# A chunked delta rule with two MoE layers on one core: four MoE pieces in place of the unused products at the first change of set, and y right behind S

## The chip, the cores and the metric

One core of a Trainium2 chip runs the whole program. The metric is the device time of one execution in microseconds (us), as the median of several runs. Its engines are TensorE (PE; PEld is its weight load), VectorE (DVE), ScalarE (ACT), GpSimd (POOL) and SyncE (SP), whose queue issues most DMAs here.

## The reference

Three stages follow each other. The first is a delta-rule attention over 4 batches x 8 heads, 768 positions of 48 values each:

```
k_n = k / (norm(k) + 1e-6);  state = 0
for t in range(S):
    y[t]  = q[t] @ state
    state = state + beta[t] * outer(k_n[t], v[t] - k_n[t] @ state)
```

Its output becomes x with 3072 rows (tokens) of 384 values. The first MoE stage is `h = ((x @ w1) * (x @ w2)) @ w3 @ w_out` with an inner width of 1024. The second is `solu = h * softmax(h)` with `h = x @ w_in`, a normalisation over the 1024 columns, and a product with `w_out`. All inputs are float32.

## The kernel before

**Chunks and sets.** The recurrence is cut into chunks of 64 positions. There are 48 chunks (64 positions of all heads of one batch), worked on in pairs (the same positions of two batches), one pair a step: 24 steps (the loop at L783), c = 2s. Four steps (8 chunks) form a set; there are six sets, 0 to 5. For every set an inverse of unit triangular matrices is needed, which VectorE builds with 62 small dependent operations between two rounds of transpositions (`invert`, L322, and `invert_end`, L343). The inverse of set n+1 is started in the second step of set n (`start_inverse`, turn 5) and goes on four operations a turn.

**A step.** `chain_u(c)` (L433) multiplies the merged inverse with V and the state and writes U over V in `X`. `chain_s(c)` (L449) adds the pair to the state in PSUM (`pst`) and copies the state into the next slot of `X`. `chain_y(c)` (L475) makes the outputs of the pair from `X` and `QA`, rounds them into the two halves of `xb`, the input of the first MoE stage, and after every second pair issues six DMAs (L499) that move the last 16 head rows of `xb` to their place. `load_v` (L421) brings V of a later pair into the same slot of `X`, which is a ring of two pairs. `merge_1`, `merge_2` and `merge_3` (L359 to L418) turn an inverse into the matrices `TW` of a pair; the functions `norm`, `prep_t` and `prep_g` (L241 to L306) normalise, transpose and multiply keys and queries of the next set. At a change of set `enter` (L762) runs the merges of the first pair of the new set.

**MoE pieces.** The first MoE stage is cut in 12 blocks of 256 tokens (`moe_block`, L566). A block is a generator with 14 pieces: 8 pieces of 18 matmuls into `pab` (128x128 by 128x256; L579), each followed by two ScalarE and two VectorE operations (L586 to L589), and 6 pieces of 12 matmuls into `px` (L603). `pab` has two PSUM buffers. `fill(x)` (L750) adds x to a counter that is capped at 3 and issues a piece for each whole unit; while the block's input isn't there yet, it issues none. A block j is let in when `y_done` reaches 4(j+1); block 0 when it reaches 6 (L738). `fill` is called eight times a step with `FT[k_]` (k_ is the step in its set; the eight calls are `turn(0)` to `turn(7)`, four ahead of `chain_s` and four behind it), and three times with `FB` = 1.4 around the merges in `enter`. What is left when the 24 steps are done runs in a tail (L882), with the conversion of the last weights between (`wog`).

**Order.** TensorE's order is the program's (`manual_schedule` at L780); the other engines' order is set by the framework's planner. `ps_prep` is a pool of four PSUM buffers that the products of the chain, the merges, the key products and y share. At the first change of set, `awake(24)` (L745) issues 24 products of the identity with itself, which nobody reads; a profile shows each as two matmuls.

The lines of the old order are these:

```
        chain_u(c)
        if s:
            chain_y(c - 2)
            y_done[0] = c
            if RX <= c + 2 < NCH:
                load_v(c + 2)
```

Of the kernel before, what the change touches and what calls it, by code (L numbers as in the profile page):

```python
# [8 lines left out]
F32 = mybir.dt.float32  # L9
# [11 lines left out]
def kernel(  # L21
# [15 lines left out]
    nc = tc.nc  # L37
# [7 lines left out]
    NCH = B * CPB  # L45
# [5 lines left out]
    TB = 256  # L51
# [3 lines left out]
    RQ, RT, RX = 16, 4, 4  # L55
# [5 lines left out]
    FB = 1.4  # L61
    FT = (0.68, 0.72, 0.8, 0.78)
    P0, C0 = 4, 24
    LO = 2
    WO, WB = 2, 15
    CPP = 2 * CPB
# [18 lines left out]
    ps_ab = ps_moe_stack.enter_context(tc.tile_pool(name="ps_ab", bufs=2, space=PSUM, side="right"))  # L85
# [7 lines left out]
    ident = const.tile([128, 128], F32, name="ident")  # L93
# [133 lines left out]
    def chunk_at(c):  # L227
        return c // CPP * 2 + c % 2, (c % CPP) // 2 * C
# [125 lines left out]
    def xcopy(c, lim):  # L354
        return nc.scalar.copy if c < lim or c >= CA and c % SETC >= SETC // 2 else nc.vector.tensor_copy
# [65 lines left out]
    def load_v(c):  # L421
        b, s0 = chunk_at(c)
        xs = slice(c % RX, c % RX + 2)
        t = v[b:b + 2].rearrange("b (p e) s d -> e s b p d", e=2)
        for h in range(2):
            nc.sync.dma_start(out=X[64 * h:64 * h + 64, xs, :, h, 0:D], in_=t[1 - h, s0:s0 + C])
        if c % CPP < 2:
            nc.gpsimd.memset(X[64:KA, xs, :, 0, 0:D], 0.0)
            nc.gpsimd.memset(X[0:D, xs, :, 1, 0:D], 0.0)
# [19 lines left out]
    def chain_s(c):  # L449
        if c % CPP >= CPP - 2:  # L450
            return
        first = c % CPP == 0
        if first:
            s_t[0] = ps_one.tile([128, 2, NP, D], F32, tag="s", name="pst")
        st, xs, xn = s_t[0], c % RX, (c + 2) % RX
        ks, sk = kst[c % RQ * 2 // RQ], c % (RQ // 2)
        for cc in range(2):

            with tc.issue_after(s_t[1].ins) if first and cc else nullcontext():
                for p in range(NP):  # L460
                    for h in range(2):
                        r = slice(64 * h, 64 * h + 64)
                        o = 64 * (1 - h)
                        mm = nc.tensor.matmul(  # L464
                            st[o:o + D, cc, p, :], ks[r, sk + cc, p, :], X[r, xs + cc, p, h, 0:D],
                            start=(first and not cc and p == 0), stop=True, skip_group_check=True,
                        )
                        if first and not cc and p == 0:
                            s_t[1] = mm
        nc.scalar.copy(out=X[64:KA, xn:xn + 2, :, 0, 0:D], in_=st[64:KA])  # L470
        conv(2 * C0, xcopy(c, CA)(out=X[0:D, xn:xn + 2, :, 1, 0:D], in_=st[0:D]))
# [3 lines left out]
    def chain_y(c):  # L475
        (qa, qs), xs = qa_of(c % RQ), c % RX
        py = ps_prep.tile([128, 2, NP, C], F32, tag="prep", name="py")
        for cc in range(2):
            for p in range(NP):
                for h in range(2):  # L480
                    o = 64 * (1 - h)
                    nc.tensor.matmul(  # L482
                        py[o:o + 64, cc, p, :], X[0:kr[h], xs + cc, p, h, :], qa[0:kr[h], qs + cc, p, h, :],
                        start=True, stop=True, skip_group_check=True,
                    )
        j = c // CPT
        if c % CPT == 0:
            xb_t[j] = moe.tile([128, 2, NP, TB], F32R, tag="xb", name="xb", bufs=2)
        xb = xb_t[j]
        hi, lo = (  # L490
            xb[:, a].rearrange("r p (b k t) -> r b p k t", b=2, k=CPT // 2)[:, :, :, c % CPT // 2, :]
            for a in range(2)
        )
        nc.scalar.copy(out=hi, in_=py)
        conv(2 * C0, nc.vector.tensor_tensor(out=lo, in0=py, in1=hi.bitcast(F32), op=ALU.subtract))
        if c % CPT == CPT - 2:
            for m in range(NM):
                for o in (0, 64):
                    nc.sync.dma_start(  # L499
                        out=xb[o + D:o + 64, :, m, :].bitcast(F32),  # L500
                        in_=xb[o + 16 * m:o + 16 * m + 16, :, NP - 1, :].bitcast(F32),
                    )
# [199 lines left out]
    def conv(x, ins=None):  # L702
        acc[0] += x
        if acc[0] < 1:
            return
        with (tc.issue_after(ins.ins) if ins is not None and c_done[0] >= CA else tc.issue_after(held[0].ins) if held[0] is not None else nullcontext()):
            while acc[0] >= 1:
                next(wg, None)
                acc[0] -= 1
# [24 lines left out]
    y_done = [0]  # L734
# [7 lines left out]
    mg = moe_all()  # L742
    owed = [0.0]

    def awake(n):  # L745
        for _ in range(n):
            pd = ps_ab.tile([128, 2, TB], F32, tag="ab", name="pd")
            nc.tensor.matmul(pd[:, 0, 0:128], ident, ident, start=True, stop=True, skip_group_check=True)

    def fill(x):  # L750
        owed[0] = min(owed[0] + x, 3.0)
        while owed[0] >= 1.0:
            if next(mg, "wait") == "wait":
                return
            owed[0] -= 1.0
# [27 lines left out]
    for s in range(NSTEP):  # L783
        c, n, k_ = 2 * s, s // PER, s % PER
        nxt = n + 1 < NSET
        if c == CD:
            drain(wg)
        b = (n + 1) * PER
        jobs = {}
        if nxt and k_ == 0:  # L790
            jobs = {
                1: lambda: prep_t(b + 1), 3: lambda: norm(b + 2),
                5: lambda: prep_t(b + 2), 7: lambda: norm(b + 3),
            }
        elif nxt and k_ == 1:
            jobs = {1: lambda: prep_t(b + 3), 5: lambda: start_inverse(n + 1)}
        elif n + 2 < NSET and k_ == PER - 1:
            jobs = {4: lambda: norm(b + PER), 7: lambda: first_keys(b + PER)}

        def turn(t):  # L800
            if t in jobs:
                jobs[t]()
            fill(FT[k_])
            for _ in range(IV):
                next(inv_gen_[0], None)

        chain_u(c)
        if s:
            chain_y(c - 2)
            y_done[0] = c  # L810
            if RX <= c + 2 < NCH:
                load_v(c + 2)
        if k_ < 2:
            merge_2(c + 2)
        if k_ == 1:
            merge_1(c + 4)
        if nxt and k_ < 2:
            prep_g(b + 2 * k_)
        for t in range(4):
            turn(t)  # L820
        chain_s(c)
        c_done[0] = c
        if k_ < PER - 1:
            merge_3(c + 2)
        if nxt and k_ < 2:
            prep_g(b + 2 * k_ + 1)
        if k_ == 0:
            merge_1(c + 4)
        if k_ == 1:
            merge_2(c + 4)  # L830
        for t in range(4, 8):
            turn(t)
        if k_ == PER - 1 and nxt:
            drain(inv_gen_[0])
            invert_end(n + 1)
            if not n:
                awake(24)
            enter(c + 2, FB)
        if c == NCH - SETC:
            prep_stack.close()  # L840
            pbw = ctx.enter_context(tc.tile_pool(name="pbw", bufs=1, side="right"))
            assert RQ == 2 * SETC and NSET % 2 == 0
            late = at.tile([128, 2 * DFF + 4 * DM], F32R, tag="QA0", name="late")
            wis = [pbw.tile([128, 2, DFF], F32R, name=f"wis{m}") for m in range(NM - 1)]
            wis.append(late[:, 0:2 * DFF].rearrange("p (a x) -> p a x", a=2))
            wig = weights_i(pbw, wis)
        if c >= NCH - SETC:
            for _ in range(NM * DFF // 256 * 6 // (SETC // 2) + 1):
                next(wig, None)
    chain_y(NCH - 2)  # L850
    y_done[0] = NCH
    while shared[0]:
        next(mg)
    pinned.__exit__(None, None, None)
# [40 lines left out]
    def b_h(i):  # L895
# [17 lines left out]
        p2 = pb2.tile([128, 1], F32, tag="p2", name="p2")  # L913
        sc = pb3.tile([128, 1], F32, tag="sc", name="sc", bufs=LO + 1)
        e = pb2.tile([128, DFF], F32, tag="e", name="e")
# [23 lines left out]
    def b_t(i):  # L939
        cen, sc = cen_t.pop(i)  # L940
        ln = pb2.tile([128, 2, NF, 128], F32R, tag="ln", name="ln", bufs=LO)
        for g in range(NF // 4):
# [21 lines left out]

    for i in range(NT128 + LO):
        if i < NT128:
# [3 lines left out]
            for _ in range(WB):  # L970
                next(wog, None)
        if i == LO:
            drain(wog)
        if i == NT128:
            b_o(i - LO)
            b_t(i - 1)
        else:
            if 0 <= i - LO:
                b_o(i - LO)
# [33 lines left out]
```

## Time and profile before

| | |
|---|---|
| median of 3 runs | 903.52 us (902.31 to 903.79) |
| the profiled execution | 905.32 us, span 903.6 us |
| TensorE busy | 827.2 us (92% of the span) |
| VectorE busy | 603.1 us (67%) |
| ScalarE busy | 451.1 us (50%) |
| mean granted TensorE clock | 0.954 of full |
| 24 steps of the recurrence | about 108 to 640 us of the span |
| tail of the first MoE stage | about 640 to 676 us |
| second MoE stage | about 676 us to the end |

Times of rows are microseconds from the start of the span, names are `out<-in`, and `L579` is line 579 of the kernel. A row of a timeline merges instructions of one line that follow each other; the bracket at its end is the time that the engine sat idle ahead of it, and what ended that. "PEclk" is the clock that TensorE was granted, as a share of full speed: 1.00 is 2.4 GHz and 0.50 is 1.2 GHz.

### The profile page before, as it was taken

Reading aid. Unit: us, or ns where it says so; the run is one execution under the profiler, and the core shown is the slowest. Engines: PE = TensorE matmul, PEld = TensorE weight load, DVE = VectorE, ACT = ScalarE, POOL = GpSimd, SP = SyncE. Lnnn points to the kernel's source line nnn. Section 1 sums busy time; section 2 is a strip of 40 time slices with the busy share of each in tenths; the row PEclk is TensorE's granted clock in tenths of the full one; section 3 lists DMA queues with packets and bytes.
Section 4 is the critical chain, followed back from the end, with each engine's and each line's share of the span. In section 5 each row is a group of like instructions: output and inputs, shape, how many; then the busy total and the mean of one; then the engine's idle time right before and its main releaser. Section 6 shows DMA issues by size and latency. Waiting matters only on the chain.

```text
span 903.6 us, 23072 instructions
## 1 busy us (share of the span) xinstructions
PE 827.2 (92%) x9536; PEld 756.9 (84%) x9536; DVE 603.1 (67%) x1472; ACT 451.1 (50%) x1081; POOL 42.5 (5%) x94
## 2 busy tenths in 40 slices
PE   4599569899998999899989999899999999999998
PEld 3355358799998999899979998799998989899997
DVE  4789884885697569856984599552566555555553
ACT  4564497346644663466345635444344433434343
POOL 5010000000000000000000000000001000000000
PEclk9699767899999999899989999899999999999999
DMA  9998513113222422232213111413232212121110
GB/s 235 270 233 148 100 26 64 28 37 88 48 63 48 84 39 63 48 78 46 63 36 81 20 54 57 132 44 107 79 95 91 70 62 70 62 70 63 56 36 32
DMA packets 140568, 70.64 MB, mean 78 GB/s; under 512 B 107056, under 2 KB 130864, under 8 KB 138672
## 3 DMA queue, kind: packets, MB, share of 16 engines
q1 hardware_dynamic: 138688, 57.64, 27.4%
q0 software_dynamic: 1776, 11.54, 3.9%
q8 instruction: 75, 1.23, 0.6%
q14 instruction: 29, 0.24, 0.1%
HBM read 47.91 MB, written 14.25 MB: 69 GB/s over the span
## 4 chain that ended last, share of the span: by engine, by line
PE 41%; issue 23%; DVE 19%; ACT 7%; DMA 5%; SPq 2%; POOL 2%; POOLq 0%; DVEq 0%; ACTq 0%
PE pab L579 13%; PE px L603 7%; PE pg L292 3%; DVE GT L339 3%; PE pu L439 3%; DVE tmp L333 3%; PE wps L552 3%; PE pw L413 2%; PE py L482 2%; SPq L499 2%; PE pst L464 1%; DVE asg L587 1%; DMA stage_a<-in_moe_w_dram 1%; PE ph L903 1%; POOL vr L933 1%
## 5 line engine op out<-in xcount | busy, mean ns | idle before, releaser
L579 PE MATMUL pab<-xb,w1s 128*128 128x256 f32 x864 | 125.7, 289 | 9.3 <-DMA xb<-xb 4.9
L579 PEld LDWEIGHTS pab<-xb,w1s 128*128 128x128 f32 x864 | 111.0, 192 | 13.3 <-DVE asg L587 5.7
L579 PE MATMUL pab<-xb,w2s 128*128 128x256 f32 x864 | 120.0, 284 | 0.0
L603 PE MATMUL px<-gh,Ws 128*128 128x256 f32 x864 | 119.0, 294 | 1.0 <-DVE gh L589 0.5
L603 PEld LDWEIGHTS px<-gh,Ws 128*128 128x128 f32 x864 | 110.5, 198 | 4.2 <-ACT gh L588 0.9
L579 PEld LDWEIGHTS pab<-xb,w2s 128*128 128x128 f32 x864 | 111.4, 193 | 0.0
L956 PE MATMUL po<-w4s,ln 128*128 128x384 f32 x432 | 79.9, 338 | 0.0
L903 PE MATMUL ph<-wis,x 128*128 128x512 f32 x288 | 76.5, 400 | 0.0
L956 PEld LDWEIGHTS po<-w4s,ln 128*128 128x128 f32 x432 | 76.2, 188 | 0.0
L588 ACT CAST gh<-asg 128x256 fp32r<-128x256 f32 x96 | 39.1, 407 | 70.7 <-DVE asg L587 70.3
L919 ACT ACTIVATE e<-ph,nm 128x1024 f32<-128x1024 f32 x24 | 26.8, 1118 | 87.4 <-DVE nm L918 85.9
L292 PE MATMUL pg<-KQ 48*64 48x128 f32 x768 | 55.4, 297 | 13.7 <-DVE KQ L274 13.7
L333 DVE TENSOR_TENSOR tmp<-D1n,GT 128x31 f32<-128x31 f32 (+15 forms) x186 | 63.3, 340 | 4.6
L339 DVE TENSOR_TENSOR GT<-GT,tmp 128x31 f32<-128x31 f32 (+15 forms) x186 | 63.3, 340 | 3.8
L587 DVE TENSOR_TENSOR asg<-pab,asg 128x256 f32<-128x256 f32 x96 | 40.4, 420 | 35.4 <-ACT asg L586 35.1
L586 ACT COPY asg<-pab 128x256 f32<-128x256 f32 x96 | 35.6, 371 | 55.3 <-PE pab L579 50.8
L292 PEld LDWEIGHTS pg<-KQ 48*64 48x64 f32 x768 | 48.4, 149 | 17.2 <-issue 10.3
L303 DVE TENSOR_TENSOR QA<-pg,mask 64x256 f32<-64x256 f32 x96 | 40.5, 422 | 32.3 <-ACT GT L300 24.9
L903 PEld LDWEIGHTS ph<-wis,x 128*128 128x128 f32 x288 | 52.4, 189 | 10.4 <-issue 0.2
L918 DVE TENSOR_REDUCE nm<-ph 128x1 f32<-128x1024 f32 x24 | 29.4, 1225 | 40.4 <-PE ph L903 40.4
L920 DVE SCALAR_TENSOR_TENSOR hs<-ph,e 128x1024 f32<-128x1024 f32 x24 | 29.4, 1225 | 30.9 <-ACT e L919 30.9
L589 DVE TENSOR_TENSOR gh<-asg,gh 128x256 fp32r<-128x256 f32 x96 | 40.5, 422 | 13.1 <-ACT gh L588 12.8
(158 smaller groups left out, 1382.3 us busy)
## 6 DMA issues: line engine op xcount, KB each, us to landing
x2d<-xs SPq DMA_DIRECT2D x36, 256.0 KB, 2.3
x<-x2d SPq DMA_DIRECT2D x24, 384.0 KB, 3.6
X<-in_v_dram SPq DMA_DIRECT2D x48, 96.0 KB, 3.1
out_dram<-ot SPq DMA_DIRECT2D x24, 192.0 KB, 1.9
ktok<-in_k_dram SPq DMA_DIRECT2D x22, 192.0 KB, 3.2
qtok<-in_q_dram SPq DMA_DIRECT2D x22, 192.0 KB, 3.3
kst<-ktok SPq DMA_DIRECT2D x88, 48.0 KB, 2.1
raw_w2s<-in_moe_w_dram POOLq DMA_DIRECT2D x4, 1024.0 KB, 8.9
```

The lines of the kernel that those rows point to most:

```text
L292: nc.tensor.matmul(pg[64 * h:64 * h + 64, p, :], KQ[r, cc, p, 0:C], KQ[r, cc, p, :], start=True, stop=True, skip_group_check=True,)
L303: nc.vector.tensor_tensor(out=qa[r, sl, :, h, :], in0=pg[r, :, C:128], in1=mask[r].unsqueeze(1).to_broadcast([64, NP, C]), op=ALU.mult,)
L333: yield nc.vector.tensor_tensor(out=t, in0=Lz[:, j, j + 1:HC].unsqueeze(2).to_broadcast([128, m, j + 1]), in1=Tt[:, j, 0:j + 1].unsqueeze( ...
L339: yield nc.vector.tensor_tensor(out=Tt[:, j + 1:HC, 0:j + 1], in0=Tt[:, j + 1:HC, 0:j + 1], in1=t, op=ALU.add)
L579: nc.tensor.matmul(pab[:, e, :], ws[m][:, a, fs], xb[:, b, m, :], start=(n == 0), stop=(n == 3 * NM - 1), skip_group_check=True,)
L586: nc.scalar.copy(out=asb, in_=pab[:, 0, :])
L587: nc.vector.tensor_tensor(out=g, in0=pab[:, 1, :], in1=asb, op=ALU.mult)
L588: nc.scalar.copy(out=gh[:, 0, f, :], in_=g)
L589: nc.vector.tensor_tensor(out=gh[:, 1, f, :], in0=g, in1=gh[:, 0, f, :].bitcast(F32), op=ALU.subtract)
L603: nc.tensor.matmul(px, Ws[:, a, f, js], gh[:, b, f, :], start=(n == 0), stop=(n == 3 * NF - 1),)
L903: nc.tensor.matmul(ph[:, gs], x2[:, m, a, :], wis[m][:, b, gs], start=(n == 0), stop=(n == 3 * NM - 1),)
L956: nc.tensor.matmul(po, ln[:, a, f, :], w4s[f][:, b, :], start=(n == 0), stop=(n == 3 * NF - 1),)
```

## The change

`chain_y(c)` moves from behind the next step's `chain_u` to right behind `chain_s(c)`; with it move `y_done` (now c + 2 there) and `load_v`, which loads the same pairs into the same slots (`c + RX`, RX = 4). The last call of `chain_y` behind the loop goes, since the loop makes all of them. `awake(24)` is replaced by two `fill(2.0)`, and in set 1 (`n == 1`) the eight calls of `fill` of a step use `F1` in place of `FT`: 20.0 units in the set instead of 23.84.

```diff
--- before.py
+++ after.py
@@ -61,6 +61,8 @@
     FB = 1.4
     FT = (0.68, 0.72, 0.8, 0.78)
     P0, C0 = 4, 24
+    EX = 2.0
+    F1 = (0.58, 0.6, 0.66, 0.66)
     LO = 2
     WO, WB = 2, 15
     CPP = 2 * CPB
@@ -742,11 +744,6 @@
     mg = moe_all()
     owed = [0.0]
 
-    def awake(n):
-        for _ in range(n):
-            pd = ps_ab.tile([128, 2, TB], F32, tag="ab", name="pd")
-            nc.tensor.matmul(pd[:, 0, 0:128], ident, ident, start=True, stop=True, skip_group_check=True)
-
     def fill(x):
         owed[0] = min(owed[0] + x, 3.0)
         while owed[0] >= 1.0:
@@ -800,16 +797,11 @@
         def turn(t):
             if t in jobs:
                 jobs[t]()
-            fill(FT[k_])
+            fill((F1 if n == 1 else FT)[k_])
             for _ in range(IV):
                 next(inv_gen_[0], None)
 
         chain_u(c)
-        if s:
-            chain_y(c - 2)
-            y_done[0] = c
-            if RX <= c + 2 < NCH:
-                load_v(c + 2)
         if k_ < 2:
             merge_2(c + 2)
         if k_ == 1:
@@ -819,6 +811,10 @@
         for t in range(4):
             turn(t)
         chain_s(c)
+        chain_y(c)
+        y_done[0] = c + 2
+        if c + RX < NCH:
+            load_v(c + RX)
         c_done[0] = c
         if k_ < PER - 1:
             merge_3(c + 2)
@@ -834,7 +830,8 @@
             drain(inv_gen_[0])
             invert_end(n + 1)
             if not n:
-                awake(24)
+                fill(EX)
+                fill(EX)
             enter(c + 2, FB)
         if c == NCH - SETC:
             prep_stack.close()
@@ -847,8 +844,6 @@
         if c >= NCH - SETC:
             for _ in range(NM * DFF // 256 * 6 // (SETC // 2) + 1):
                 next(wig, None)
-    chain_y(NCH - 2)
-    y_done[0] = NCH
     while shared[0]:
         next(mg)
     pinned.__exit__(None, None, None)
```

## Rows read from the trace of the kernel before

**Rows 1.** Stretches: from:to, length, busy (instructions) of PE, PEld, DVE, ACT, POOL; clock; DMA.

```profile
108.00:163.40 55.40, 40.71 (x796) 36.81 (x794) 35.78 (x70) 44.45 (x109) 0.96 (x1) 0.68 0.27 52
...
205.60:294.90 89.30, 85.22 (x1363) 81.54 (x1362) 65.81 (x164) 49.20 (x131) 0.96 (x1) 1.00 0.27 59
294.90:569.20 274.30, 260.85 (x4045) 249.10 (x4044) 200.29 (x501) 146.43 (x393) 3.70 (x5) 0.98 0.25 58
```

**Rows 2.** Timeline of TensorE: start, length, instructions, in brackets the wait and its releaser.

```profile
134.31 3.68 PE L292 MATMUL pg<-KQ 48*64 48x128 f32 x32 [6.23 <-DVE KQ L274]
...
163.48 0.45 PE L439 MATMUL pu<-X,TW 112*64 112x48 f32 x2 [0.68 <-ACT TW L417]
...
167.70 1.77 PE L579 MATMUL pab<-xb,w1s 128*128 128x256 f32 x9
...
173.62 1.34 PE L579 MATMUL pab<-xb,w1s 128*128 128x256 f32 x9 [0.92 <-DVE asg L587]
...
188.75 7.48 PE L748 MATMUL pd<-ident 128*128 128x128 f32 x48
196.16 0.69 PE L368 MATMUL pm<-Dt,G 32*32 32x32 f32 x32
...
198.86 0.60 PE L392 MATMUL pm<-xp,D1n 32*32 32x32 f32 x26 [0.38 <-DVE xp L376]
```

**Rows 3.** Timeline of VectorE: start and last transposition of two inversions.

```profile
158.01 1.93 DVE L323 STREAM_TRANSPOSE D1n<-GT 128x1024 f32<-128x1024 f32 x1
...
193.33 1.96 DVE L344 STREAM_TRANSPOSE Dt<-GT 128x1024 f32<-128x1024 f32 x1
...
245.88 2.08 DVE L323 STREAM_TRANSPOSE D1n<-GT 128x1024 f32<-128x1024 f32 x1
...
277.92 2.08 DVE L344 STREAM_TRANSPOSE Dt<-GT 128x1024 f32<-128x1024 f32 x1
```

**Rows 4.** Timeline of TensorE at the three later changes of set.

```profile
282.73 0.65 PE L267 MATMUL pk<-ident,ktok 128*128 128x128 f32 x4 [2.38 <-DVE ktok L251]
...
285.91 0.69 PE L368 MATMUL pm<-Dt,G 32*32 32x32 f32 x32
...
376.80 0.86 PE L392 MATMUL pm<-xp,D1n 32*32 32x32 f32 x26 [2.24 <-DVE xp L376]
...
469.41 0.90 PE L392 MATMUL pm<-xp,D1n 32*32 32x32 f32 x26 [3.01 <-DVE xp L376]
```

**Rows 5.** Waits of TensorE for `xb`: the total, the longest (timeline).

```profile
PE pab L579 <- DMA xb<-xb: 4.9, 7, 1.4
...
576.38 0.59 PE L579 MATMUL pab<-xb,w1s 128*128 128x256 f32 x3 [1.44 <-DMA xb<-xb]
```

**Rows 6.** Stretches, columns as in Rows 1: three of those at half clock.

```profile
161.90:168.70 6.80, 5.95 (x86) 5.46 (x81) 5.14 (x17) 2.84 (x6) 0.00 (x0) 0.50 0.14 29
376.90:383.70 6.80, 6.80 (x88) 6.65 (x87) 3.10 (x9) 1.11 (x3) 0.00 (x0) 0.50 0.26 66
...
578.30:585.10 6.80, 6.15 (x78) 5.65 (x76) 2.19 (x8) 2.32 (x6) 0.00 (x0) 0.50 0.52 161
```

**Rows 7.** Chain that ended last: two ab pieces, 24 px products twice, a chain product.

```profile
205.68 1.12 PE pu L439 x32
...
235.50 4.32 PE pab L579 x36
...
289.25 3.06 PE px L603 x24
...
378.49 5.39 PE px L603 x24
```

**Rows 8.** Writes of the converted w2: last two (range of starts).

```profile
L224 DVE TENSOR_TENSOR w2s<-raw_xb,w2s x2: 687/689/691, 130.3 to 131.9; 128x512 fp32r<-128x512 f32 x2
```

**Rows 9.** Waits of the SP queue: V loads for y's product.

```profile
SPq L426 <- PE py L482: 89.4, 11, 18.7
```

## The prediction

> **What bounds the kernel now.** I read the table of stretches first [rows 1]: after 163.4 us TensorE is busy 85.22 of 89.3 us in the second set of chunks and 260.85 of 274.3 us in the next three, so it is the bound, and a change pays by what it takes from TensorE's work or its pauses. Then the timeline of TensorE around the first change of set [rows 2]: the 48 unused products run from 188.75 until the merge at 196.16 (7.4 us), the first MoE piece starts at 167.70, and chain_u(6) ahead of it waited 0.68 us. Third, VectorE [rows 3]: the inversion of the second set runs from 158.01 to the transposition at 193.33 (done at 195.3), that of the third from 245.88 to 277.92 (done at 280.0). Fourth, TensorE's waits at the later changes of set [rows 4], the waits for the 16 head rows that DMAs move inside `xb` [rows 5], and the stretches at half clock, 1.2 GHz: the one until 168.7, and three of 6.8 us later, of which the first and the last stand in [rows 6].
>
> **Prices.** A piece of the first kind (18 products; "ab") takes 4.32/2 = 2.16 us, one of the second (12; "px") 3.06/2 = 1.53 us, a chain product of 32 small matmuls 1.1 us [rows 7].
>
> **Pieces, counted by hand from `fill`'s counter.** A block is 8 ab and 6 px. Before: 8 pieces in the fourth step, 4 at the first change of set: 12 when set 1 (the second) begins; 24 + 4 in it: 40; then 28 a set, and 20 in the tail. After: block 0's gate opens inside the third step, since `y_done` is 6 there: 5 pieces in that step, 6 in the fourth, 4 for the two `EX` fills, 4 around the merges: 19. Set 1 issues 20 + 5: 44. From there on 28 a set, and 16 in the tail. At every change of set the three fills give 2, 1, 2 instead of 1, 2, 1. The first piece finds its operands: `w2s` is last written at 131.9 [rows 8], and `xb` of block 0 is sent on a step earlier than now.
>
> **Set 0.** Out go 7.4 us of unused products. y of a pair now stands behind its S. In the first step it lies in a wait of 6.23 us for VectorE [rows 2], so I cost it at nothing; were that cover gone, it would be 1.9 us at half clock. In the second it precedes the key products, and VectorE's inversion starts 1.0 us later. Third step: y's 1.9 us stand where chain_u(6) stands now (163.48, less its 0.68 of waiting), so the first piece starts at 163.48 - 0.68 + 1.0 + 1.9 = 165.7. Five ab are 10.8 us; half clock until 168.7 [rows 6], if it stays, adds 1.5; one wait for VectorE of 0.9, as at 173.62 [rows 2], and chain_u(6) starts at 178.9. Then 1.1 for it, three ab 6.5, S and y 2.0, two px 3.1, key transpositions 1.0, a px 1.5, and for the `EX` fills three px and an ab 6.8: the merge comes at 200.9 instead of 196.16. The inversion is done by then (195.3 + 1.0, and 0.3 for one more px result), so VectorE isn't late. Four ab instead of four px around the merges, less a wait of 0.38: +2.1. Set 1 begins **6.8 us later, seven pieces ahead**. The five pieces may instead each wait 0.9 for VectorE's in-order queue, where inversion steps stand ahead of their results: 0 to 4.5; I take 0.9, as the eight pieces of today had one such wait.
>
> **Set 1.** Up to the start of its inversion: six ab and two px today, three ab and four px after, 16.0 - 12.6 = 3.4 us less, and 0.45 for a wait on `xb` that goes: inversion start +2.95. In the inversion VectorE has four ab results and one px result fewer, some 1.5 us: done at 280.0 + 2.95 - 1.5 = 281.4. TensorE's pieces beside it fall from 10 ab and 6 px (30.8) to 8 and 5 (24.9), so it runs out at 277.4, 278.4 with the transpositions: **a new wait of 3.0 us for VectorE**. The merge then stands at 281.4; today it stands at 285.91, because key normalisation was queued behind the transpositions (2.38 us [rows 4]) and a piece followed. At the other changes the normalisation came earlier, so I take -4.5; if it stays behind, -0.8. Then three px and two ab around the merges instead of four px, +2.8. A wait of 2.24 brought half clock at 376.9 [rows 4, 6], one of 2.38 at 282.73 none: I take it: 6.8/2 = 3.4 (0 to 3.4). Set 2 begins at -4.5 + 2.8 + 3.4 = **+1.7**, four pieces ahead (two px, two ab, **-7.4**).
>
> **Later sets.** The waits for `xb` are 4.9 us in all [rows 5]; 0.45 is counted, 4.4 are left, the longest (1.44) at 576.4. After, the blocks concerned start behind the merges, with y a half step earlier: **-4.4**. Two waits ahead of the second merge product, 2.24 and 3.01 [rows 4], get a second px (1.53) as cover, and the pieces just before leave VectorE fewer results; but what is late next is VectorE's transposition itself, so I take half of 5.25 less 0.6: **-2.3** (0 to -5.2). The half clock behind those waits costs up to half of TensorE's busy time in it, 3.4 in the first, 3.1 in the last [rows 6], some 9.7 in all three; two begin at such a wait, the third in the `xb` waits. I take half: **-5.0** (0 to -9.7).
>
> The half clock is real in this trace: 24 px products take 5.39 us behind 376.9 and 3.06 elsewhere [rows 7]. The Trainium skill ("TensorE: Matmul & The Clock Gate", the caveats in Part 1) warns that clock events of a trace have been unreliable. By that warning the clock terms (-5.0 and +3.4) would go and the sum be -14.8; the durations speak against it.
>
> **Tail.** 16 pieces instead of 20 are already in the four ahead. The conversion of the last weights is as long as now, interleaved with fewer pieces: 0 to +3, I take **+1.0**.
>
> **DMA queues.** y's six `xb` copies and two V loads (and two small POOL fills once) move half a step forward on SP. V loads hold SP today for 89.4 us in eleven waits on y's product [rows 9], with key loads and x2d stores queued behind; after, they are issued right behind that product, so the wait can't grow by more than the half step, which is covered by a set's lead of the key loads: 0.
>
> **Sum** against the profiled execution (span 903.6, 905.3 in all, 1.8 above the median of the three runs): +1.7 - 7.4 - 4.4 - 2.3 - 5.0 + 1.0 = -16.4, so 888.9 beside its 905.3, and **887.1** on the scale of the median. A measurement of this kernel can tell about 0.2% (1.8 us) from no change. The bounds above make the forecast's own range 879 to 898.
>
> **Rivals.**
> 1. *VectorE sets each set's length* (0.10): every inversion starts a fixed time after the last, freed TensorE time turns into waiting. For: VectorE has hardly a pause from 158 to 195; the new wait in set 1. Against: it is busy 200.29 of 274.3 us later [rows 1], and today TensorE ends each inversion busy. Then set 0's +6.8 stays, four px leave the tail (-6.1): 904.2, no change.
> 2. *The clock falls in the third step and through set 1* (0.12): two `pab` buffers cycle against a full VectorE queue, TensorE pauses a little at every piece and drops to 1.2 GHz. Each stretch like those of [rows 6] costs 3.4; from the fifth on (16.4/3.4) the change loses. With eight, some 54 us of the 130 there, +27: 914, slower. For: with few products in the first steps the mean level was 0.68 [rows 1]. Against: set 1 ran at 1.00. The Trainium skill describes such a fall under PSUM buffers that cycle ("TensorE: Matmul & The Clock Gate", "A second HAM failure mode: psum-queue depth-cycling"); this trace shows none with these two buffers.
> 3. *The early pieces wait* (0.10) for `xb` until 167.7 and for VectorE at each piece: +2.0 + 3.6: 892.7.
> 4. *All named waits and half-clock stretches go* (0.07): another -2.3 - 5.0 - 3.4: 876.4.
>
> That the pieces aren't issued is excluded by the count of the gate above.
>
> **Chances.** Forecast 0.61; with 3 and 4, faster 0.78; rival 1, same 0.10; rival 2, slower 0.12. The range, 877 to 904.5, leaves out rivals 2 and 4 (0.19).
>
> **What would show it.** Right: first `pab` near 166, nineteen pieces ahead of set 1's chain_u, which stands near 212.4; a wait of about 3 us at the second change of set; no wait on `xb` near 575; fewer half-clock stretches after 370; 16 pieces in the tail. Wrong: set lengths from set 2 on as today (rival 1), or half clock between 166 and 280 (rival 2). A first piece that waits long for its data, or y that holds up the first two steps, would break the set 0 part.

## The result, and the profile after

The changed kernel takes **879.56 us** (median of 5 runs, 877.84 to 881.55) beside 903.52: ratio 0.974, 95% interval 0.9722 to 0.9759, faster by 24 us. The forecast was 887.1 in a range of 877.0 to 904.5: the sign and the range held, the number was 7.5 us too long. The profiled execution after took 877.84 us with a span of 876.1 (before 905.32 and 903.6), so its trace shows 27.5 us. Every trace below is one execution: up to set 1 b_lag3 runs the code of before, and yet its trace begins set 1 at 203.3 where that of before does at 205.6. In the changed file lines behind L64 stand 2 further down, up to the lines of the change.

The stretches of after, columns as in rows 1: sets 0, 1, 2 to 4, then set 5 with the tail, and two stretches for the clock. Behind them two of before: the first chain_u of its set 5 starts at 568.55, 0.65 us ahead of the cut in rows 1.

```profile
115.20:208.40 93.20, 80.60 (x1234) 75.83 (x1234) 70.57 (x168) 57.14 (x144) 0.96 (x1) 0.87 0.23 48
208.40:291.40 83.00, 80.11 (x1309) 75.76 (x1308) 62.71 (x158) 47.25 (x125) 0.95 (x1) 1.00 0.29 61
291.40:550.60 259.20, 255.46 (x4041) 244.69 (x4040) 196.88 (x497) 146.42 (x391) 3.70 (x5) 1.00 0.27 61
550.60:648.60 98.00, 94.53 (x1222) 91.73 (x1222) 55.70 (x146) 46.25 (x117) 0.00 (x0) 0.98 0.30 90
166.80:640.70 473.90, 463.87 (x7033) 444.94 (x7031) 346.25 (x884) 256.15 (x673) 4.65 (x6) 1.00 0.28 66
640.70:644.10 3.40, 3.32 (x19) 3.13 (x20) 3.02 (x9) 1.23 (x3) 0.00 (x0) 0.68 0.01 4
```

```profile
294.90:568.55 273.65, 260.50 (x4041) 248.88 (x4040) 200.00 (x500) 145.78 (x392) 3.70 (x5) 0.98 0.25 58
568.55:676.00 107.45, 103.60 (x1313) 100.66 (x1314) 57.50 (x147) 48.69 (x121) 0.00 (x0) 0.97 0.30 89
```

Set 1 began 2.8 us later than before (208.4 beside 205.6), took 83.0 us instead of 89.3, sets 2 to 4 took 259.2 instead of 273.65, set 5 and the tail 98.0 instead of 107.45: +2.8 - 6.3 - 14.45 - 9.45 = -27.4. The second MoE stage kept its length. In sets 2 to 4 TensorE's idle time fell from 13.15 to 3.74 us (-9.4) and its busy time by 5.0, for the same 4041 instructions: that is the clock, at full rate from 166.8 to 640.7, where before had three stretches at half [rows 6].

Timeline of TensorE after, the lines that answer to rows 2, 4 and 5:

```profile
126.11 1.15 PE L484 MATMUL py<-QA,X 112*64 112x64 f32 x32 [1.48 <-ACT KQ L271]
131.74 1.95 PE L415 MATMUL pw<-TW,kst 64*48 64x64 f32 x32 [4.48 <-DVE QA L305]
133.48 3.51 PE L294 MATMUL pg<-KQ 48*64 48x128 f32 x32
...
163.90 1.40 PE L581 MATMUL pab<-xb,w1s 128*128 128x256 f32 x9
...
174.95 1.14 PE L441 MATMUL pu<-X,TW 112*64 112x48 f32 x32
...
196.59 0.69 PE L370 MATMUL pm<-Dt,G 32*32 32x32 f32 x32
...
208.45 1.14 PE L441 MATMUL pu<-X,TW 112*64 112x48 f32 x32
...
247.68 0.59 PE L581 MATMUL pab<-xb,w1s 128*128 128x256 f32 x3 [0.66 <-DMA xb<-xb]
...
279.45 0.69 PE L370 MATMUL pm<-Dt,G 32*32 32x32 f32 x32 [0.80 <-DVE Dt L346]
...
456.65 0.60 PE L394 MATMUL pm<-xp,D1n 32*32 32x32 f32 x26 [1.11 <-DVE xp L378]
...
566.98 1.34 PE L581 MATMUL pab<-xb,w1s 128*128 128x256 f32 x9 [1.99 <-DVE asg L589]
...
640.56 1.82 PE L605 MATMUL px<-gh,Ws 128*128 128x256 f32 x9 [1.41 <-ACT gh L590]
```

Five pieces run from 163.90 to 174.95 without a pause. The merge of the first change of set stands at 196.59, where it stood before (196.16 in rows 2), with seven more pieces done. Only one wait for `xb` is left, and the wait at the second change of set is 0.80 us. TensorE's waits by releaser, from 165 to 648.6 (us in total, times, longest; before: `xb` 4.9 in seven [rows 5], and at the second merge product 2.24 and 3.01 in rows 4):

```profile
PE pab L581 <- DVE asg L589: 4.3, 5, 2.0
PE pm L394 <- DVE xp L378: 1.6, 2, 1.1
PE pm L370 <- DVE Dt L346: 1.5, 2, 0.8
PE pab L581 <- DMA xb<-xb: 0.7, 1, 0.7
```

The SP queue of after, answering to rows 9: the V loads wait longer for y than before, and the run a_loadv below shows that nobody pays for it.

```profile
SPq L428 <- PE py L484: 102.3, 17, 21.1
```

### The profile page after: what moved, and what is told of

Same layout as the page of the kernel before. It is cut to its first block, busy times and chain, and to the rows that moved or that the text cites. A ratio compares the mean times of both kernels' runs of the same rounds, so it can differ in the third digit from the quotient of the medians.

```text
span 876.1 us, 22962 instructions
## 1 busy us (share of the span) xinstructions
PE 812.4 (93%) x9488; PEld 743.1 (85%) x9488; DVE 600.0 (68%) x1472; ACT 451.5 (52%) x1081; POOL 42.4 (5%) x94
## 4 chain that ended last, share of the span: by engine, by line
PE 45%; issue 23%; DVE 18%; ACT 6%; DMA 5%; POOL 2%; SPq 0%; POOLq 0%; DVEq 0%; ACTq 0%
PE pab L581 16%; PE px L605 8%; PE pg L294 4%; DVE GT L341 3%; PE pw L415 3%; DVE tmp L335 3%; PE pu L441 2%; DMA stage_a<-in_moe_w_dram 2%; PE py L484 2%; PE wps L554 2%; PE pst L466 2%; PE ph L898 1%; POOL vr L928 1%; DMA st_o<-in_moe_w_out_dram 1%; PE pm L394 1%
## 5 line engine op out<-in xcount | busy, mean ns | idle before, releaser
L581 PE MATMUL pab<-xb,w1s 128*128 128x256 f32 x864 | 123.7, 288 | 4.9 <-DVE asg L589 4.3
L605 PE MATMUL px<-gh,Ws 128*128 128x256 f32 x864 | 113.9, 289 | 1.5 <-ACT gh L590 1.4
L605 PEld LDWEIGHTS px<-gh,Ws 128*128 128x128 f32 x864 | 107.1, 193 | 3.4 <-ACT gh L590 1.6
L554 PE MATMUL wps<-area 128*128 128x384 f32 x128 | 45.0, 503 | 2.6 <-DVE Ws L226 1.8
```

What stands on the lines that cost most here:

```text
L554: nc.tensor.matmul(acc[m], w3t[:, j, :], wos[kk // (NF // 2)][:, kk % (NF // 2), :], start=(kk == 0), stop=(kk == NF - 1),)
L581: nc.tensor.matmul(pab[:, e, :], ws[m][:, a, fs], xb[:, b, m, :], start=(n == 0), stop=(n == 3 * NM - 1), skip_group_check=True,)
L605: nc.tensor.matmul(px, Ws[:, a, f, js], gh[:, b, f, :], start=(n == 0), stop=(n == 3 * NF - 1),)
```

## The experiments

Each kernel was timed beside the kernel before on the same chip. Differences between two kernels are of their medians; by the ratios they come out up to 3 us otherwise. In the table, "ahead" is the count of pieces issued when set 1 ends, worked out from `fill`'s counter and found in the timelines; "fills" the pieces around the merges at most changes of set from the second on (before gives 2, 1, 1 at the last, fill_lag at the second). "Distance" is worked out from each timeline: from the end of y's products of a block's last pair to the block's first product, waiting included; the shortest of the second and third block, then of all later ones. "Half" is the time at half clock from 190 us to the end of the first MoE stage: twice (1 - granted clock) x 3.4 us, summed over slices of 3.4 us. "Sets 2 to 4" is from chain_u to chain_u.

| kernel | y | ahead | fills | distance | xb waits | half | sets 2 to 4 | ratio |
|---|---|---|---|---|---|---|---|---|
| before | old | 40 | 1,2,1 | 6.3 / 5.1 | 4.9 | 20.4 | 273.7 | 1 |
| b_first | old | 40 | 2,1,1 | 6.3 / 5.1 | 5.2 | 6.8 | 269.7 | 0.995 |
| b_lag3 | old | 37 | 1,2,1 | 10.5 / 10.4 | 0.9 | 10.2 | 267.7 | 0.989 |
| fill_alone | old | 40 | 1,2,1 | 4.4 / 4.9 | 9.1 | 27.3 | 272.2 | 1.002 |
| fill_lag | old | 38 | 2,1,2 | 4.5 / 8.1 | 6.0 | 10.2 | 262.9 | 0.990 |
| y_alone | new | 43 | 2,1,1 | 10.4 / 8.7 | 0 | 6.8 | 262.4 | 0.980 |
| a_empty | new | 40 | 2,1,2 | 16.5 / 17.3 | 0 | 13.7 | 260.4 | 0.983 |
| **after** | new | 44 | 2,1,2 | 6.3 / 8.7 | 0.7 | 3.4 | 259.2 | 0.974 |
| a_121 | new | 44 | 1,2,2 | 6.3 / 8.7 | 0.4 | 10.2 | 267.5 | 0.979 |
| a_gate | new | 40 | 1,2,1 | 14.9 / 15.1 | 0 | 3.4 | 268.6 | 0.994 |
| a_lead6 | new | 46 | 2,1,2 | 5.3 / 4.6 | 5.1 | 10.2 | 271.0 | 0.992 |
| a_nof1 | new | 47 | 2,1,1 | 5.2 / 4.2 | 25.6 | 54.4 | 299.5 | 1.034 |

**What the table says of sets 2 to 4**, where every kernel issues 84 pieces (y_alone, fill_lag and a_nof1 85): two things set their length. One is the distance: at fills of 1, 2, 1 it takes 273.7 to 267.7 us (before to b_lag3, 6.0 us). Only 1.4 us of that are waits for `xb`, and b_lag3's three pieces fewer also shift which pieces stand beside the merges, so the 6.0 are distance and shift together; fill_alone and a_gate, with the same pieces in the same places, differ by 3.6. The other thing is whether one or two pieces stand ahead of the second merge product: 267.5 to 259.2 at equal distance and with the same pieces (a_121 to after, 8.3 us). Together 273.7 - 6.0 - 8.3 = 259.4, and after has 259.2. Beyond the distance, y's place doesn't appear: with two pieces and no waits for `xb` there it is 262.9 with y in its old place (fill_lag) and 262.4 in the new (y_alone). With one piece it stays at 268.6 even where y is moved and every block starts late (a_gate).

**y_alone: y moved, with its `y_done` and `load_v`, the rest as before.** The unused products stay, `FT` holds everywhere.

```diff
-            chain_y(c - 2)
...
         chain_s(c)
+        chain_y(c)
+        y_done[0] = c + 2
```

> y moved behind S, but the 24 unused products stay and every set uses FT: 15 pieces ahead of set 1 instead of 19, 17 in the tail instead of 16, and the fills at a change of set give 2, 1, 1. Theory A (the parts add up: the unused products' 7.4 us at the first change; everything after it comes from y's place and the count of the first fill): no waits on xb, merge waits as in the changed kernel, full clock from about 175 us on, so the changed kernel's 879.6 plus the 7.4 us that the unused products take, some 886 to 889. Theory L (the lead of four pieces from the first change of set is what shortens the later sets): the later sets keep their waits and half-clock stretches, 896 to 902.

Measured: 887.03 us beside 903.26, ratio 0.9795 (0.9764 to 0.9826). Theory A held: y's move alone brings most of the gain. In its sets 2 to 4 no wait for `xb` is left and the clock is full, and at the merges it waits (us in total, times, longest):

```profile
PE pm L394 <- DVE xp L378: 2.7, 3, 1.6
```

**fill_alone: the four pieces and F1, y in its old place.**

```diff
-            fill(FT[k_])
+            fill((F1 if n == 1 else FT)[k_])
...
-                awake(24)
+                fill(EX)
+                fill(EX)
```

> The two fills of 2.0 and F1 in set 1, with y in its old place behind the next chain_u. By the counter block 1 isn't let in at the first change of set, so the fills there give 2, 2 and 1, 1, 0: 14 pieces ahead of set 1, 40 at its end as before, 20 in the tail, 1, 2, 1 at the later changes. Theory A: the 7.4 us of unused products go, two pieces more (3.1 us) stand at the first change of set and two fewer in set 1; the waits on xb (4.4), the merge waits (5.2) and the three half-clock stretches (9.7) stay: 895 to 898. Theory L: with no lead at the end of set 1, nothing but the unused products is gained, the same 895 to 898; a result under 890 would mean that the later gains don't need y's move.

Measured: 905.64, ratio 1.0022 (1.0003 to 1.0041): the expectation missed, no gain at all. The second block now begins right behind its own y; the start of set 1 in its timeline, and its waits for `xb`:

```profile
205.07 1.11 PE L484 MATMUL py<-QA,X 128*64 128x64 f32 x31
...
210.60 0.59 PE L581 MATMUL pab<-xb,w1s 128*128 128x256 f32 x3 [1.91 <-DMA xb<-xb]
211.85 0.63 PE L581 MATMUL pab<-xb,w1s 128*128 128x256 f32 x3 [0.66 <-DMA xb<-xb]
213.13 0.79 PE L581 MATMUL pab<-xb,w1s 128*128 128x256 f32 x3 [0.66 <-DMA xb<-xb]
```

```profile
PE pab L581 <- DMA xb<-xb: 9.1, 10, 1.9
```

y ends at 206.18, the last of the copies that the piece needs has landed at 213.13: the piece waits three times, for one part of its input after the other.

**b_first: the kernel before with fills 2, 1, 1 around the merges.**

```diff
+        w = (2.0, 1.0, 1.2) if x else (0.0, 0.0, 0.0)
-        fill(x)
+        fill(w[0])
...
```

> The kernel before, with the three fills around the merges 2.0, 1.0, 1.2 instead of 1.4 each: they give 2, 1, 1 at every change of set instead of 1, 2, 1; totals per set unchanged. Theory A (a second px piece ahead of the second merge product covers VectorE's transposition and copies): the waits of 2.24 and 3.01 us shrink by 1.53 each and the half clock behind them goes (6.6): 892 to 896. Theory B (the waits go only where the pieces ahead of the merges leave VectorE fewer results, as in the changed kernel where they are px and not ab): a second px delays nothing but the pause, VectorE is as late, and the wait moves to the third merge: 901 to 904.

Measured: 899.94 beside 903.26, ratio 0.9949 (0.9931 to 0.9968). Between the two expectations: the second piece ahead of the second merge product is worth 3.3 us by itself (4.0 in sets 2 to 4), and the waits for `xb` stay (5.2).

**a_121: after with fills 1, 2, 2.**

```diff
-        fill(x)
+        fill(w[0])
...
+        w = (1.0, 2.0, 1.2) if x else (0.0, 0.0, 0.0)
```

> The changed kernel, with the fills around the merges 1.0, 2.0, 1.2: they give 1, 2, 1 at the first change of set and 1, 2, 2 at the others instead of 2, 1, 1 and 2, 1, 2; totals per set unchanged. Theory A: the first fill covers 1.5 us less, waits of 1.5 to 2.5 us come back at three or four changes of set, and half clock with some of them: 885 to 893. Theory B: VectorE has fewer results to make ahead of the merges, waits grow by under 1 us each and the clock stays: 880 to 884.

Measured: 884.95, ratio 0.9785 (0.9768 to 0.9802), 5.4 us above after, at the lower end of theory A. At the third change of set, timeline and stretch (columns as in rows 1):

```profile
369.32 0.60 PE L394 MATMUL pm<-xp,D1n 32*32 32x32 f32 x26 [1.47 <-DVE xp L378]
```

```profile
372.40:375.80 3.40, 3.40 (x45) 3.27 (x44) 0.56 (x2) 0.37 (x1) 0.00 (x0) 0.66 0.62 104
```

After has no wait at this merge product and no half clock here. The wait of 1.47 us is back with one px fewer ahead of it, and a stretch of half clock behind it, at this and the next two changes of set.

**a_gate: after, but the gate of the blocks (`y_done`) opens where it did before.** y itself stays in its new place.

```diff
         chain_u(c)
+        y_done[0] = c
...
         chain_y(c)
-        y_done[0] = c + 2
```

> The changed kernel, with y and the V loads where the change puts them, but y_done is set where it was set before (behind the next chain_u, to c). By the counter block 0 is let in a half step later again (8 pieces in the fourth step, none in the third), block 1 not at the first change of set (2, 2 and then 1, 1, 0), 40 pieces at the end of set 1, 20 in the tail. Theory G (what y's move gives is the earlier letting in of blocks): the result is that of the fills without y's move, 900 to 906. Theory P (what it gives is y's place: xb half a step earlier, so no waits for it): the 4.4 us of xb waits and the half clock behind them go, the merge waits stay, 894 to 899.

Measured: 895.62 beside 902.33, ratio 0.994 (0.9919 to 0.9961); theory P held. No wait for `xb` is left (every block but the first starts 14.9 us or more behind its y), and only 3.4 us of half clock, but in its sets 2 to 4, 268.6 us long, TensorE still waits:

```profile
PE pm L394 <- DVE xp L378: 4.0, 3, 2.3
PE pq L274 <- ACT GT L302: 2.2, 3, 0.8
PE pk L269 <- DVE ktok L253: 2.1, 1, 2.1
```

Beside fill_alone (905.64), which issues the same pieces in the same places, a_gate differs by y and the V loads alone, and the V loads cost nothing (next run): y's place is worth 10 us (7 by the ratios) at the same pieces, and with the longer distance the 9.1 us of waits for `xb` go. What it allows is worth 16 more: pieces issued half a step earlier, four more of them by the end of set 1, and with them a counter that stands so that the first fill at a change of set gives two pieces and not one.

**a_loadv: after, with the V loads in their old place.**

```diff
         chain_u(c)
+        if RX <= c + 2 < NCH:
+            load_v(c + 2)
...
-        if c + RX < NCH:
-            load_v(c + RX)
```

> The changed kernel, with the V loads back behind the next step's chain_u; y stays right behind S. Theory A: V arrives a set of steps ahead of its use, the loads' place costs nothing: 879 to 881. Rival Q (the SP queue was held up by V loads that wait for y's product, with key loads and stores behind them; part of the gain is that queue): 883 to 888.

Measured: 878.91, ratio 0.9747 (0.9725 to 0.9768): the same as after. The place of the V loads costs nothing.

**a_empty: after without the four pieces, and without the unused products.**

```diff
-            if not n:
-                fill(EX)
-                fill(EX)
```

> The changed kernel without the two fills of 2.0: nothing stands at the first change of set between the last piece and the first merge. F1 stays, so set 1 issues 20 + 5 pieces from 15: 40 at its end, 20 in the tail. Theory A: TensorE waits for VectorE's transposition, some 4 us, the four pieces (6.8 us) are issued in the tail, the set is shorter by what isn't waited for, and the wait may bring one half-clock stretch (3.4): 883 to 888. Rival E (an empty first change of set lets the clock fall for longer, as in the first steps, and set 1 starts at half clock): 889 to 896.

Measured: 885.85, ratio 0.9828 (0.9794 to 0.9861), 6.3 us above after. The first change of set in its timeline:

```profile
197.26 1.06 PE L370 MATMUL pm<-Dt,G 32*32 32x32 f32 x32 [4.39 <-DVE Dt L346]
```

Without the pieces TensorE waits 4.39 us, and the clock is at half from then on (some 6.8 us here, and again at 282.4 with a wait of 2.47). The times of the two merges, 197.26 here and 196.59 in after, can't be compared as they stand, since VectorE ended its inversion 2.3 us later here; its last transposition in after, and here:

```profile
192.73 2.07 DVE L346 STREAM_TRANSPOSE Dt<-GT 128x1024 f32<-128x1024 f32 x1
```

```profile
195.20 1.91 DVE L346 STREAM_TRANSPOSE Dt<-GT 128x1024 f32<-128x1024 f32 x1
```

In after the four pieces run from 190.0 to 196.6, and the transposition ends at 194.8: some 4.8 of their 6.6 us lie beside the inversion, 1.8 behind it. a_gate has 40 pieces ahead as well: a_empty, without the four, is 9.8 us below it by the earlier gate and the fills 2, 1, 2, and the four pieces bring the other 6.3 of the 16 us.

**a_nof1: after with `FT` in set 1 too.** 47 pieces ahead instead of 44, 13 in the tail.

```diff
-            fill((F1 if n == 1 else FT)[k_])
+            fill(FT[k_])
```

> The changed kernel, with FT in set 1 as in the other sets, so the four pieces of the two fills come out of the tail and not out of set 1: 47 pieces at the end of set 1, 13 in the tail, fills at the changes 2, 1, 1. Theory A: a piece costs the same in set 1 and in the tail, and the tail still covers the last conversion: 879 to 883. Rival S (set 1 is short of VectorE, so four pieces more beside its inversion bring a longer wait at its end and half clock): 884 to 889.

Measured: 932.96, ratio 1.0343 (1.0311 to 1.0374). Both theories missed, the nearer one by 44 us. Waits for `xb`, a row of the timeline, and stretches of its set 1 and of its sets 2 to 4:

```profile
PE pab L581 <- DMA xb<-xb: 25.6, 25, 2.9
```

```profile
254.24 2.12 PE L581 MATMUL pab<-xb,w2s 128*128 128x256 f32 x9
```

```profile
253.40:256.80 3.40, 3.34 (x16) 3.37 (x16) 2.98 (x10) 0.62 (x2) 0.95 (x1) 0.50 0.00 0
310.60:610.10 299.50, 275.14 (x4061) 260.40 (x4060) 202.59 (x509) 149.07 (x398) 3.70 (x5) 0.94 0.24 55
```

The pieces have caught up with y: nearly every block starts 4 to 8 us behind its input's products and waits for the copies. Sets 2 to 4 have 24.4 us idle, 16.0 of them for `xb`, and in all 54 us of the kernel run at half clock, where nine products take 2.12 us instead of 1.24. A wait of some 5 us a set comes with a set that is 13 us longer than after (with one piece more in the three).

After this the theory was new: what counts is the distance between a block's y and its first piece, and y's move works by making it longer. The next two kernels change that distance by `F1` alone, once in either direction; a_gate had already changed it at the same order of pieces.

**b_lag3: the kernel before, three pieces fewer in set 1.**

```diff
+    F1 = (0.58, 0.62, 0.72, 0.68)
...
-            fill(FT[k_])
+            fill((F1 if n == 1 else FT)[k_])
```

> The kernel before with F1 = (0.58, 0.62, 0.72, 0.68) in set 1 alone: three pieces fewer there (37 issued at its end instead of 40, so 23 in the tail instead of 20), y in its old place, the unused products and the fills 1, 2, 1 as before. Every block from set 2 on starts three pieces (some 6 us) later behind the six copies of its input. Theory A (it is the distance between a block's y and its first piece that counts, wherever y stands): the waits for xb, 4.9 us in seven, fall under 1.5, and the half clock near 578, which stands behind the longest of them, goes: 903.5 - 4.0 - 3.1 = 896, so 894 to 899. Theory B (the place of y itself brings the gain, by what it moves out of the way of chain_u): the waits on xb may go, but nothing else, and three more pieces stand in the tail: 901 to 905.

Measured: 891.24 beside 901.60, ratio 0.9886 (0.9861 to 0.991): theory A, and more than it gave. One line of constants brings 10 us to the old kernel, without moving y. Its waits for `xb`, and sets 2 to 4 (columns as in rows 1):

```profile
PE pab L580 <- DMA xb<-xb: 0.9, 2, 0.6
```

```profile
289.10:556.80 267.70, 257.02 (x4042) 245.83 (x4042) 201.07 (x504) 147.31 (x396) 3.70 (x5) 0.99 0.26 61
```

The 0.9 us are of the first block. Of the 6.0 us that sets 2 to 4 lose, 3.5 are busy time (half clock that went) and 2.5 idle time; most of the waits at the merges (3.9 of 5.3 us for xp) stay. The half clock near 578 went with the waits for `xb` there, as theory A had it.

**a_lead6: after, two pieces more in set 1.**

```diff
-    F1 = (0.58, 0.6, 0.66, 0.66)
+    F1 = (0.63, 0.65, 0.735, 0.735)
```

> The kernel after with F1 = (0.63, 0.65, 0.735, 0.735): 46 pieces issued at the end of set 1 instead of 44, 14 in the tail instead of 16. Theory A (the distance between y and the first piece of its block counts, and it falls step by step): one block a set now starts right behind its y, so a wait of 1 to 2 us for xb a set and some half clock come back: 879.6 + 4 x 1.5 + 2 to 6 = 884 to 892, between the kernel after (879.6) and the one with seven pieces ahead (933). Theory B (only when every block starts right behind its y do the waits feed on one another): 878 to 881.

Measured: 894.1, ratio 0.9919 (0.9893 to 0.9944). Theory A's direction, 2 us beyond its range. Waits from 210 to 663 us:

```profile
PE pk L269 <- DVE ktok L253: 5.4, 3, 2.1
PE pab L581 <- DMA xb<-xb: 5.1, 9, 0.9
```

Of the 14.5 us above after, 4.4 are waits for `xb`, and some 3.4 the additional half clock; the 5.4 us for the key normalisation on VectorE, which theory A had not, are most of the rest. Why VectorE is late there was not tried.

**fill_lag: fill_alone with three pieces fewer in set 1**, which keeps the later blocks 8 us or more behind their y.

```diff
-    F1 = (0.58, 0.6, 0.66, 0.66)
+    F1 = (0.53, 0.56, 0.6, 0.6)
```

> The kernel before, y in its old place, with the four pieces in place of the unused products and with F1 = (0.53, 0.56, 0.6, 0.6): 38 pieces at the end of set 1 (fill_alone had 40, the kernel after has 44), 67 and then 28 more a set, 22 in the tail; the fills at the changes of set are 2, 1, 2 from set 2 on, as after. It differs from the kernel after by y's place, and the first piece of a block comes 8 us or more behind its y, as there. Theory A (all that y's new place brings is that distance, which can be had as well by issuing fewer pieces in set 1): no waits on xb but the one in set 0, half clock under 7 us in all, 880 to 887, near the kernel after (879.6). Theory B (y's place pays by itself too, by what follows chain_u at once and by when VectorE gets y's results): 889 to 897, near b_lag3 (891.2), the waits for xp and GT as before (7 us together).

Measured: 893.34 beside 901.99, ratio 0.9903 (0.9881 to 0.9926). The time is theory B's, its reason isn't: from set 2 on the waits for xp and GT are gone with y in its old place. Sets 2 to 4, and the second block:

```profile
295.40:558.30 262.90, 255.31 (x4054) 244.55 (x4053) 201.51 (x505) 147.49 (x395) 3.70 (x5) 1.00 0.27 61
```

```profile
210.43 0.59 PE L581 MATMUL pab<-xb,w1s 128*128 128x256 f32 x3 [1.98 <-DMA xb<-xb]
```

262.9 us beside 259.2 after and 273.7 before: with fills as after, distances in these sets no shorter and one piece more, three quarters of that gain come without moving y. Most of what is missing lies outside: the second and third block (4.5 and 7.3 us behind their y) wait 5.3 us in set 1, which takes 92.2 us instead of 83.0, and six more pieces are left for the tail. That is what y's new place gives: the same lead in pieces at a longer distance, in sets 0 and 1.

**a_spread: after, the conversion of the last weights spread over the steps.**

```diff
+            if c > NCH - SETC:
+                next(wig, None)
+                next(wig, None)
...
-    WO, WB = 2, 15
+    WO, WB = 1, 15
```

> The kernel after with the conversion of the last weights spread over the turns of the last set of steps (two operations of it at each turn) instead of a burst behind every step, and in the tail one operation a piece instead of two. Theory A (the bursts on VectorE and ScalarE make the two waits of the trace of after for asg at 566.98, 1.99 us, and for gh at 640.56, 1.41 us, and the one half-clock stretch behind the second, worth 1.7): 879.6 - 1.5 to - 4.5, so 875 to 878. Theory B (the conversion's work on VectorE and ScalarE only moves, and other pieces wait in its place): 878.5 to 882.

Measured: 879.62, ratio 0.9756 (0.9728 to 0.9784): no difference from after, theory B. The two waits are still there:

```profile
571.32 1.55 PE L581 MATMUL pab<-xb,w1s 128*128 128x256 f32 x9 [3.60 <-DVE asg L589]
...
645.93 4.32 PE L605 MATMUL px<-gh,Ws 128*128 128x256 f32 x31 [1.22 <-ACT gh L590]
```

That the first is 3.60 here and 1.99 in after says nothing of the spreading: a_loadv, with the conversion as in after and the same time, waits 3.50 there (568.46). No version beat the changed kernel.

## Why the prediction was right, and by what it missed

**Pieces and prices** held: five pieces ahead of chain_u(6), six px and an ab between its S and the merge, 2.2 us an ab (11.05/5), seven more than before when set 1 begins.

**Size of the miss.** By the two traces the sum is 11.0 us short (16.4 of 27.4): 5.2 in sets 0 and 1, 4.8 in the later sets, 1.0 in the tail. 3.5 of it are the two executions (27.5 us apart, the medians 24.0).

**Set 0: +6.8 predicted, +2.8 measured.** Three terms of the sum fell away: the first piece came at 163.90 instead of 165.7, no wait for VectorE stood in the five pieces (0.9), and the clock was up by then, so the 1.5 us of half clock weren't paid. 1.8 + 0.9 + 1.5 = 4.2. Part of this is the execution and not the kernel: a_lead6, a_nof1 and a_spread, the same code up to set 1, start their first piece at 165.9 to 167.0 and set 1 at 210.4 to 211.5, 4.8 to 5.9 us later than the trace of before. Of the work that was called free, y(0) stands ahead of a wait that no row of before had: 4.48 us at 131.74, ahead of merge_3's product. Behind it the wait of 6.23 us of rows 2 is gone, so the cost of nothing stood.

**Set 1: the new wait was 0.80 us instead of 3.0, and no half clock followed (3.4 taken).** The 3.0 came of a slip in the count. Among today's pieces beside the inversion the sum has ten ab, but the tenth starts behind the wait of 2.38 us at 282.73 [rows 4], from whose start, 280.35, the sum counts (280.35 + 2.95 - 5.9 = 277.4):

```profile
283.58 1.32 PE L579 MATMUL pab<-xb,w1s 128*128 128x256 f32 x9
```

With nine ab and six px, 28.6 us, the pieces fall by 3.7 and not by 5.9: TensorE runs out at 279.6, at 280.6 with the transpositions, and up to 281.4 the prediction's own numbers leave a wait of 0.8 us. The merge came at 279.45 instead of 281.4: set 1 had begun 4.0 us earlier than forecast, but the inversion took 34.3 us (from 244.97) and not 32.6, so the 1.5 us that fewer results were to save VectorE did not show (34.1 before). Set 2 then began 3.5 us earlier than before, not 1.7 later. Of longer waits at this merge, 1.95 us (b_lag3) and 2.47 (a_empty) came with half clock, 2.30 (fill_lag) and 3.16 (a_gate) did not.

**The waits for `xb`: right.** 4.4 us were to go in the later sets, and all of them went; the one left is in set 1. But this term stood for more than its waits: the half clock near 578 went too, and y's move at the same pieces, from fill_alone to a_gate, brings 7 to 10 us.

**The merges: 2.3 us taken, 3.0 went** in sets 2 to 4 (of 5.25 for xp 1.6 are left, and 0.7 for Dt are new). a_121 shows what the second px ahead of that product is worth with the clock that hangs on it: 8.3 us in sets 2 to 4, the larger of the two effects there (4.0 in b_first, at the short distance).

**Half clock: 5.0 taken, 6.4 went.** The sum took half of 9.7. All three stretches went, and one of 3.4 us came back in the tail: 5.0 us less busy time in sets 2 to 4, 3.1 less 1.7 in set 5 and the tail. The Trainium skill ("TensorE: Matmul & The Clock Gate", the caveats in Part 1) warns that clock events of a trace may be unreliable; here the trace speaks against it, by the 5.0 us just named and by the 2.12 us for nine products in a_nof1.

**Not in the sum at all** were shorter waits in sets 2 to 4: for GT (2.1 to 0), asg (3.0 to 1.4), TW and gh (1.4 to 0), 5.1 us together. The waits for asg (1.99) and gh (1.41) in set 5 and the tail, which the sum didn't have either, took 3.4 back.

**Tail:** -7.4 for the four pieces and -1.4 for the clock make -8.8 of the 9.45 measured, without the +1.0.

**The rivals.** Rival 4 came nearest (876.4 for 879.56). Rival 1 fell: each later set is 4 to 5 us shorter. Rival 2's fall of the clock in set 1 didn't come in after, but a_nof1 shows that state three pieces away (0.94 in sets 2 to 4), by pieces that wait for DMAs, not by VectorE's queue. Rival 3's waits didn't come.

**What the prediction did not see** is that the parts don't add. y alone -16 us, the pieces with F1 alone +2, together -24; and `F1`, counted as work that changes places, is what keeps the 24 us from turning into a loss of 30 (a_nof1). No term of the sum said how far ahead is too far: 46 pieces already cost 14.5 us (a_lead6). That the change stops at 44 was luck as far as the sum goes. Whether y's products gain a little by standing behind S in sets 0 and 1, at equal distances there, no run separates: fill_lag has the shorter ones in set 1. Which of VectorE's results comes late when a block begins at another place of the set (the key normalisation of a_lead6) was not followed up.

## What to carry to other kernels

When two streams are interleaved by counters, compute for each block the distance between its producer and its first consumer, and compare it with the latency of the transfer between: here blocks that started 8.66 us or more behind waited for nothing, and three more pieces of lead turned a gain of 24 us into a loss of 30. When a forecast counts the work beside another engine, check for each piece in the timeline on which side of the wait it stands: one piece on the wrong side made 0.8 us into 3.0. A stretch at half clock goes with the wait ahead of it, but a wait need not bring one, so give it a chance and not a fixed price.

## What the runs showed of the hardware that was not expected

- The rounding and the six copies inside `xb` take 7 to 10 us from the end of y's products: the wait for the last part of a block's input ended 6.95 us behind them in fill_alone (206.18 to 213.13), 8.1 in after, 9.8 in fill_lag's third block and 10.3 at the most (a_nof1, 495.25). fill_lag's block that started 8.10 us behind still waited 0.64 for its last part; no block that started at 8.66 us or later waited. In fill_alone the parts of the input came 1.25 to 1.28 us after one another (210.60, 211.85, 213.13).
- TensorE fell from 2.4 to 1.2 GHz with waits of 1.30 us (b_lag3 at 457.30), 1.47 (a_121 at 369.32), 1.95 (b_lag3 at 276.58) and 2.47 (a_empty at 282.36), and did not with 1.99 (after at 566.98) and 3.16 (a_gate at 282.74). The 2.47 and the 3.16 us stand at the same merge, the second change of set; here the row and the stretch behind it (columns as in rows 1), first of a_empty, then of a_gate, where the granted clock was 0.50 and 1.00:

```profile
282.36 1.07 PE L370 MATMUL pm<-Dt,G 32*32 32x32 f32 x32 [2.47 <-DVE Dt L346]
282.70:286.10 3.40, 3.40 (x40) 3.34 (x36) 3.36 (x6) 3.06 (x8) 0.00 (x0) 0.50 0.52 102
```

```profile
282.74 0.69 PE L370 MATMUL pm<-Dt,G 32*32 32x32 f32 x32 [3.16 <-DVE Dt L346]
282.70:286.10 3.40, 2.31 (x44) 2.09 (x44) 3.37 (x5) 2.12 (x6) 0.00 (x0) 1.00 0.66 131
```

One short wait can so cost up to 3.4 us beyond itself (a stretch of 6.8 us at half clock), and the 25.6 us of waits for `xb` in a_nof1 come with 54 us at half clock, which cost some 27 more. What tells the two cases apart, these runs do not show.
